# Another table of ranks for the list scheduler of an attention and two feed-forward blocks

## Chip, cores and metric

The kernel runs on one core of one Trainium2 chip, as one launch. The metric is the device time of one execution in microseconds (us); lower is better. TensorE (PE) does the matrix products, ScalarE (ACT), VectorE (DVE) and GpSimd (POOL) everything elementwise, and SyncE (SP) issues most of the DMAs.

## The reference, cut to what matters

Three stages follow each other. B=4 batches, H=8 heads, S=1152 positions, D=64; after attention the 4 x 576 rows of 512 numbers go through two feed-forward blocks.

```
q_pool = q.reshape(B, H, 576, 2, D).mean(axis=3)
p      = softmax(q_pool @ k.T / sqrt(D))
x      = (p @ v) as [2304, 512]
y      = (s * relu(x @ w_in) ** 2 + b) @ w_out               # 512 -> 2048 -> 512
out    = (sigmoid(y @ w_gate) * (y @ w_val)) @ w_out2        # 512 -> 1536 -> 512
```

The weights arrive as 64-bit floats (two 32-bit words each), everything else as 32-bit floats.

## The kernel before, in words

Products are made to keep the precision of 32-bit floats: an operand is split into a "hi" part that TensorE takes whole and a "lo" part, the rest. So nearly every product has a hi and a lo operation ahead of it on ACT, DVE or POOL, and a feed-forward product is three matmuls (lines 538 to 540: hi*hi, hi*lo, lo*hi).

Batch 0's attention is done by rows (`pair_rows`; operations named "r ...", prepared by "pr ..."): scores with queries on the partitions, row maximum and exponential from PSUM, then transposes of the probabilities. Batches 1 to 3 are done by columns (`pair_half`; prepared by "ps ..."). There one head's half goes through this chain: nine score products "qk" (line 768), for each a copy to SBUF "s copy" on ACT and a running maximum "s max" on DVE, three transposes "max T" (line 781), the reduction "max" (DVE, line 785), its way back to rows "max rows" (PE, line 746), three times "s - max" (DVE) and "exp" (ACT, line 794), the split "p hi" (ACT or POOL, lines 462 and 464) and "p lo" (DVE or POOL, line 472), and the products with v: "pv hi" (lines 816 and 817, six matmuls) and "pv lo" (line 821).

The first feed-forward block (`ffn1`) runs batch by batch: "ff xx up", "ff relu", "square", "g hi", "g lo", "ff down", "ff y add". For batch 0 its weights are decoded from 64-bit words: "w load" (DMA), "w top" (POOL or DVE), "w scale" (ACT), "w low", "w join", "w sign" (DVE), "w hi" (ACT or POOL), "w lo" (DVE or POOL). The result is kept in DRAM ("w keep"), and batches 1 to 3 fetch it by a DMA that POOL issues ("w fetch", line 520). The second block (`ffn2`: "p2 yy up", "gate", "gate val", "h hi", "h lo", "down 2", "out", "out add", "out store") handles two batches at a time, opens once the last attention tile is stored ("turn"), and decodes its weights both times. It stands in the order ffn2 of batches 0 and 1, ffn1 of batch 3, ffn2 of batches 2 and 3.

The order of all of it is made on the host, before the launch, by a list scheduler (`Plan`). Each operation is added with its engine (or a choice of two engines), an assumed duration, what it reads and writes, the buffers it needs, and a rank. `Plan.order` then runs an assumed clock: whenever an engine is free, it takes, among the operations on it whose inputs are ready and whose buffers fit, the one with the lowest rank. The program is issued in the order that comes out, and each engine then executes its own list strictly in that order.

```
FE, DE, AT, SK, FP = 0, 0.5, 1, 2, 3
...
up, on = self.moved.get(name, (0, 0))
self.ops.append([alts, None, issue, (rank + up, i + on), after, slots, port])
...
for item in items:
    if at[item[1]] <= now and (best is None or item < best) and fits(ops[item[1]]):
```

`rank` is one of the five constants: FE for the elementwise work of the feed-forward blocks, DE for decoding in ffn1 (FE in ffn2), AT for attention up to the exponentials, SK for what follows them, FP for feed-forward products. To it the table `MOVED` adds its first number for that name; its second shifts the place in program order that breaks ties. `self.moved` is that table. Operations that may run on either of two engines ("p hi", "p lo", "w lo", "g hi" and others) go to the one that reaches them first.

Of the kernel before, what the change touches and what calls it, by code (L numbers as in the profile page):

```python
# [25 lines left out]
    w=4, raw=3, xy=2, xx=1, r=2, g=4,  # L26
    qn=1, kn=1, vn=1, qT=2, kT=2, vt=2, st=6, pp=6,
    sg=2, mx=2, mc=2, r9=1, x=1, s=2, rs=1, rr=1,
    yy=1, yl=1, h=4, fo=9,
    ps=4, pr=8, pm=1, acc=5, ff=6, p2=3, bank=8,  # L30
# [5 lines left out]


MOVED = {
    "q load": (-0.5, 114),
    "k load": (46, 79),  # L40
    "v load": (58.5, 89),
    "v hi": (-18, -97),
    "v lo": (60, -156),
    "q add": (0, -97),
    "q twice": (0, -7),
    "pr qT": (0, 53),
    "pr q hi False": (23, -93),
    "pr q lo False": (24.5, 3),
    "pr q hi True": (45.5, 50),
    "pr q lo True": (5, 36),  # L50
    "pr kT": (-5, 44),
    "pr k hi": (2, -112),
    "pr k lo": (-5, 116),
    "s b load": (15, 94),
    "r qk 1": (0, 35),
    "r max": (36, 97),
    "r - max": (-29, -40),
    "r exp": (60, -57),
    "r pT": (-23, 13),
    "r p": (0, 52),  # L60
    "r p hi": (17, -107),
    "r p lo": (-25.5, -51),
    "r pv": (-38, 107),
    "r pT hi": (0, 70),
    "r pT lo": (47, -75),
    "r o": (-40, 39),
    "r x add": (40, -62),
    "r qk 2": (-1.5, -71),
    "r sums": (0.5, 106),
    "r sums eps": (-4, 9),  # L70
    "r 1 / sums": (-8, 75),
    "r spread": (-38, 44),
    "r rows": (0, -92),
    "r rows mid": (0, 108),
    "r x / sums": (-1.5, 74),
    "r x / sums mid": (60, 35),
    "r end": (0, 96),
    "ps qT": (24, 13),
    "ps q hi False": (60, 90),
    "ps q lo False": (6, -123),  # L80
    "ps kT": (10, 16),
    "ps k hi": (36.5, -29),
    "ps k lo": (-1, 88),
    "xx hi": (58, -86),
    "xx lo": (2.5, 93),
    "w load": (-12, 6),
    "w top": (-17, 81),
    "w scale": (-3, 17),
    "w low": (-20.5, -68),
    "w join": (9, 116),  # L90
    "w sign": (-25.5, -42),
    "w hi": (-40, 42),
    "w lo": (-28.5, -87),
    "w keep": (-1, 29),
    "one": (-39, -96),
    "ff xx up": (58, 135),
    "ff relu": (0, 72),
    "square": (-40, 76),
    "g hi": (27.5, -76),
    "g lo": (-10.5, 98),  # L100
    "ff down": (57, 43),
    "ff y": (9, 84),
    "column sum": (0, -65),
    "ff y add": (15.5, 115),
    "bias": (13.5, -34),
    "y bias": (-3, 137),
    "y store": (-33, -12),
    "qk": (44.5, 68),
    "s copy": (34.5, 24),
    "s max": (14, 33),  # L110
    "max T": (0, 53),
    "max": (20.5, 103),
    "max rows": (41.5, -120),
    "s - max": (14.5, 67),
    "exp": (0, -7),
    "p hi": (-40, -44),
    "p lo": (-7.5, -102),
    "pv hi": (-10.5, -118),
    "pv lo": (49.5, -31),
    "sums": (41, -60),  # L120
    "x": (36.5, 0),
    "sums out": (10, -13),
    "sums in": (5, -102),
    "1 / sums spread": (-16.5, 16),
    "1 / sums out": (60, -32),
    "1 / sums in": (2.5, -82),
    "x / sums": (0, 63),
    "1 / sums": (27.5, -20),
    "w fetch": (-35.5, -18),
    "w come": (-20.5, 6),  # L130
    "x store": (44, -24),
    "turn": (20, -21),
    "yy load": (-40, -79),
    "yy hi": (0, 50),
    "yy lo": (0, -39),
    "p2 yy up": (4.5, 6),
    "gate": (8, -90),
    "gate val": (-25.5, -72),
    "h hi": (0.5, 90),
    "h lo": (-40, -43),  # L140
    "down 2": (-21, 31),
    "out": (-5, -6),
    "out add": (0, -59),
    "out store": (-2, 45),
    "xx load": (0, 48),
    "p2 xx up": (0, -49),
    "p2 relu": (0, -7),
    "p2 down": (0, 24),
    "p2 y": (-10, -68),
    "p2 y add": (40, -54),  # L150
}


# [991 lines left out]
```

## Time and profile before

| | us |
|---|---|
| median of 3 runs | 1452.34 (1451.93 to 1453.6) |
| the profiled execution's own time | 1457.94 |
| its span, first to last instruction | 1456.2 |
| TensorE matmul busy | 1381.1 (95%) |
| VectorE, ScalarE, GpSimd busy | 1069.8, 936.4, 762.1 |
| mean granted TensorE clock | 0.990 of full speed |

The trace covers one execution, so its numbers are set against 1457.94 us and not against the median. Work is counted as busy time of each engine; "idle before, and what ended it" is the time an engine stood before an instruction, and the instruction of another engine that released it. In the tables by stretch each engine has its busy time and, in brackets, its instructions; PEclk is the granted clock as a share of 2.4 GHz.

### The profile page before, as it was taken

The page shows a single profiled execution, that of the slowest core. Times are in us where ns is not written, and L with a number is a line of the kernel's source. Part 1 is how long each engine was busy: PE and PEld are TensorE (multiplying, and loading weights), DVE is VectorE, ACT ScalarE, POOL GpSimd, SP SyncE. Part 2 cuts the span into 40 slices and gives each one's busy share as a digit, 9 for nine tenths or more (in the row PEclk, how much of TensorE's full clock was granted, in tenths as well). Part 3 has the DMA queues.
Part 4 walks back from the last instruction along what each step waited for, and adds up shares of the span by engine and source line. Part 5 has one row for each costly group of instructions (what it writes and reads, how often), then busy time and mean ns, then how long its engine had stood idle before and what let it go on. Part 6 is the DMA issues. An engine that isn't in the chain of part 4 may idle for free.

```text
span 1456.2 us, 24999 instructions
## 1 busy us (share of the span) xinstructions
PE 1381.1 (95%) x9164; PEld 1315.3 (90%) x9164; DVE 1069.8 (73%) x1780; ACT 936.4 (64%) x2004; POOL 762.1 (52%) x664
## 2 busy tenths in 40 slices
PE   7988999888999999999999989999999999999998
PEld 6877989887888999999899989999898999989897
DVE  6899899888998889889998856747475126738552
ACT  6899889778798999888888735434141534434130
POOL 3678577667776557565755434525353004526230
PEclk9999999999999999999999999999999999999999
DMA  3336134454433342233341363312236444313112
GB/s 90 93 121 200 31 101 124 155 157 149 154 109 136 87 140 75 84 103 121 95 140 42 121 260 131 101 59 87 73 100 230 163 172 145 117 48 126 34 69 65
DMA packets 103043, 167.88 MB, mean 115 GB/s; under 512 B 44652, under 2 KB 80264, under 8 KB 93832
## 3 DMA queue, kind: packets, MB, share of 16 engines
q1 hardware_dynamic: 96008, 115.95, 25.9%
q0 software_dynamic: 6912, 50.33, 9.8%
q8 instruction: 72, 1.18, 0.3%
q14 instruction: 51, 0.42, 0.1%
HBM read 139.99 MB, written 26.28 MB: 114 GB/s over the span
## 4 chain that ended last, share of the span: by engine, by line
PE 50%; ACT 8%; DVE 4%; issue 3%; DMA 2%; POOL 2%; SPq 0%; DVEq 0%; POOLq 0%; ACTq 0%
PE banks L538 11%; PE banks L540 11%; PE banks L539 11%; PE banks L1047 3%; PE banks L1048 3%; PE banks L1046 3%; PE banks L768 3%; ACT st L794 2%; PE banks L816 1%; ACT st L469 1%; PE banks L821 1%; PE banks L817 1%; DVE mx L475 1%; ACT pp L462 1%; DMA w<-d_1u_1u 1%
## 5 line engine op out<-in xcount | busy, mean ns | idle before, releaser
L472 POOL TENSOR_TENSOR pp<-st,pp 128x864 fp32r<-128x864 f32 x82 | 174.9, 2137 | 42.4 <-ACT pp L462 31.6
L540 PE MATMUL banks<-yy,w 128*128 128x384 f32 x576 | 192.6, 334 | 0.3 <-POOL w L472 0.3
L538 PE MATMUL banks<-yy,w 128*128 128x384 f32 x576 | 192.5, 334 | 0.0
L539 PE MATMUL banks<-yy,w 128*128 128x384 f32 x576 | 192.5, 334 | 0.0
L469 ACT COPY st<-banks 128x288 f32<-128x288 f32 x432 | 151.3, 409 | 39.9 <-PE banks L768 32.4
L768 PE MATMUL banks<-qT,kT 128*128 128x288 f32 x864 | 161.4, 304 | 3.2 <-DVE mx L475 2.7
L475 DVE TENSOR_TENSOR mx<-banks,mx 128x288 f32<-128x288 f32 x336 | 150.7, 449 | 18.1 <-ACT st L469 7.0
L538 PE MATMUL banks<-xx,w 128*128 128x288 f32 x512 | 155.1, 303 | 8.1 <-DMA w<-d_1u_1u 5.1
L539 PE MATMUL banks<-xx,w 128*128 128x288 f32 x512 | 152.4, 298 | 0.0
L540 PE MATMUL banks<-xx,w 128*128 128x288 f32 x512 | 152.4, 298 | 0.0
L475 DVE TENSOR_TENSOR st<-st,banks 128x864 f32<-128x864 f32 x144 | 148.9, 1043 | 2.4 <-PE banks L746 1.5
L538 PE MATMUL banks<-g,w 128*128 128x288 f32 x448 | 135.1, 302 | 3.3 <-DVE mx L475 2.1
L794 ACT ACTIVATE st<-st 128x864 f32<-128x864 f32 x144 | 132.0, 927 | 7.0 <-DVE st L475 6.4
L496 POOL TENSOR_SCALAR raw<-raw 128x512 f32<-128x512 f32 x99 | 77.4, 782 | 109.1 <-DMA raw<-in_moe_w_out_dram 40.6
L816 PE MATMUL banks<-pp,vt 128*128 128x288 f32 x432 | 123.6, 306 | 11.0 <-ACT pp L462 7.3
L768 PEld LDWEIGHTS banks<-qT,kT 128*128 128x128 f32 x864 | 127.9, 190 | 6.0 <-DVE mx L475 4.2
L539 PE MATMUL banks<-g,w 128*128 128x288 f32 x448 | 132.5, 296 | 0.0
L540 PE MATMUL banks<-g,w 128*128 128x288 f32 x448 | 132.5, 296 | 0.0
L817 PE MATMUL banks<-pp,vt 128*64 128x288 f32 x432 | 119.8, 297 | 0.0
L499 ACT ACTIVATE raw<-raw 128x512 f32<-128x512 f32 x104 | 71.1, 685 | 71.8 <-POOL raw L496 66.0
L540 PEld LDWEIGHTS banks<-yy,w 128*128 128x128 f32 x576 | 108.1, 188 | 0.6 <-POOL w L472 0.6
L538 PEld LDWEIGHTS banks<-yy,w 128*128 128x128 f32 x576 | 108.1, 188 | 0.3
(147 smaller groups left out, 3952.4 us busy)
## 6 DMA issues: line engine op xcount, KB each, us to landing
w<-d_1u_1u POOLq DMA_DIRECT2D x24, 1024.0 KB, 5.6
w<-d_1d_1d POOLq DMA_DIRECT2D x24, 1024.0 KB, 6.6
raw<-in_moe_w_out_dram SPq DMA_DIRECT2D x40, 512.0 KB, 3.9
raw<-in_moe_w_gate_dram SPq DMA_DIRECT2D x24, 512.0 KB, 12.7
raw<-in_moe_w_val_dram SPq DMA_DIRECT2D x24, 512.0 KB, 3.8
qn<-in_q_dram SPq DMA_DIRECT2D x16, 576.0 KB, 3.7
kn<-in_k_dram SPq DMA_DIRECT2D x32, 288.0 KB, 3.9
vn<-in_v_dram SPq DMA_DIRECT2D x32, 288.0 KB, 2.8
```

Source lines behind the costliest of these rows:

```text
L469: act(name, n, lambda: nc.scalar.copy(out=out(), in_=in_()), r, w, rank, sbuf=False)
L472: shared(name, n, lambda e: ENGINE[e].tensor_tensor(out=out(), in0=in0(), in1=in1(), op=op), r, w, rank, 2.15)
L475: dve(name, n, lambda: nc.vector.tensor_tensor(out=out(), in0=in0(), in1=in1(), op=op), r, w, rank)
L496: shared("w top", 512, lambda e: ENGINE[e].tensor_scalar(out=words(1).bitcast(F32), in0=words(1).bitcast(F32), scalar1=F64_TOP, scalar2=-F ...
L499: act("w scale", 512, lambda: nc.scalar.mul(words(1).bitcast(F32), words(1).bitcast(F32), 2.0 ** -112), [], [top], rank)
L538: nc.tensor.matmul(ps(), lhsT=whi(), rhs=xhi(), start=first, stop=False)
L539: nc.tensor.matmul((ps_lo or ps)(), lhsT=whi(), rhs=xlo(), start=False, stop=False)
L540: nc.tensor.matmul(ps(), lhsT=wlo(), rhs=xhi(), start=False, stop=last)
L768: nc.tensor.matmul(ps.t[:, :HQ], lhsT=kT.t[:, c], rhs=qq[:, w, hf * HQ:(hf + 1) * HQ], start=(w == 0), stop=(w == 1))
L794: act("exp", 3 * HQ, lambda s=s: nc.scalar.activation(out=s.t, in_=s.t, func=AF.Exp), [], parts, AT)
L816: nc.tensor.matmul(acc.t[:, :HQ], lhsT=vt.t[:, 3 * i + c, D:], rhs=hi.t[:, c], start=(i == c == 0), stop=False)
L817: nc.tensor.matmul(acc.t[:D, :HQ], lhsT=vt.t[:, 3 * i + c, :D], rhs=hi.t[:, c], start=False, stop=False)
```

## The change

All 112 entries of `MOVED` get other numbers; nothing else in the file changes. The same operations with the same tiles, engines to choose from and assumed durations go through the same scheduler, which may put them in another order and give an operation with a choice to the other engine. The entries that the prediction speaks of:

```diff
-    "pr k lo": (-5, 116),
+    "pr k lo": (-24, -69),
-    "ps q lo False": (6, -123),
+    "ps q lo False": (14.5, 47),
-    "ps kT": (10, 16),
+    "ps kT": (-1, 40),
-    "ps k hi": (36.5, -29),
+    "ps k hi": (23.5, -20),
-    "xx lo": (2.5, 93),
+    "xx lo": (29, 103),
-    "w load": (-12, 6),
+    "w load": (-40, -115),
-    "w lo": (-28.5, -87),
+    "w lo": (-31, 33),
-    "ff xx up": (58, 135),
+    "ff xx up": (60, -47),
-    "ff down": (57, 43),
+    "ff down": (33.5, 15),
-    "ff y add": (15.5, 115),
+    "ff y add": (18.5, 36),
-    "qk": (44.5, 68),
+    "qk": (15, -59),
-    "s copy": (34.5, 24),
+    "s copy": (28, 30),
-    "s max": (14, 33),
+    "s max": (11, -75),
-    "max T": (0, 53),
+    "max T": (-40, 58),
-    "max": (20.5, 103),
+    "max": (39, 59),
-    "s - max": (14.5, 67),
+    "s - max": (32, 49),
-    "p hi": (-40, -44),
+    "p hi": (-17.5, -87),
-    "pv hi": (-10.5, -118),
+    "pv hi": (-32.5, -57),
-    "pv lo": (49.5, -31),
+    "pv lo": (32, 66),
-    "1 / sums": (27.5, -20),
+    "1 / sums": (-5, 0),
-    "w fetch": (-35.5, -18),
+    "w fetch": (-34, 14),
-    "yy load": (-40, -79),
+    "yy load": (0, 68),
-    "xx load": (0, 48),
+    "xx load": (-3, 54),
...
```

## Rows read from the trace of the kernel before

**Rows 1.** The profile's first two lines: the span, and busy time by engine.

```profile
span 1456.2 us, 24999 instructions
...
PE 1381.1 (95%) x9164; PEld 1315.3 (90%) x9164; DVE 1069.8 (73%) x1780; ACT 936.4 (64%) x2004; POOL 762.1 (52%) x664
```

**Rows 2.** Busy time by stretch, with granted clock and DMA.

```profile
core 0: us, PE busy (x) PEld busy (x) DVE busy (x) ACT busy (x) POOL busy (x), PEclk, DMA share, GB/s
0.00:40.00 40.00, 29.86 (x181) 26.92 (x181) 26.40 (x61) 26.82 (x79) 14.56 (x26) 0.96 0.31 82
40.00:480.00 440.00, 395.35 (x2825) 370.53 (x2825) 391.59 (x735) 379.47 (x886) 312.68 (x274) 0.98 0.41 129
480.00:840.00 360.00, 350.12 (x2611) 339.19 (x2611) 315.06 (x513) 309.79 (x642) 212.21 (x157) 1.00 0.32 100
840.00:880.00 40.00, 36.22 (x262) 36.02 (x261) 20.75 (x30) 14.57 (x27) 15.52 (x16) 0.96 0.64 241
880.00:1440.00 560.00, 558.27 (x3243) 533.30 (x3242) 312.13 (x436) 205.19 (x370) 207.09 (x193) 1.00 0.33 109
1440.00:1456.20 16.20, 11.33 (x53) 9.38 (x51) 3.88 (x6) 0.51 (x1) 0.00 (x0) 0.96 0.35 81
```

**Rows 3.** What TensorE waited for: us in total, times, longest us.

```profile
PE banks L816 <- ACT pp L462: 7.3, 10, 2.0
PE banks L746 <- DVE mc L785: 7.2, 8, 2.7
PE banks L702 <- ACT qn L462: 6.7, 1, 6.7
...
PE banks L538 <- DMA w<-d_1u_1u: 5.1, 2, 3.8
PE banks L538 <- DVE mx L475: 4.3, 2, 2.2
PE banks L816 <- POOL pp L464: 3.4, 3, 1.5
PE banks L781 <- DVE mx L475: 2.9, 6, 1.1
PE banks L768 <- DVE mx L475: 2.7, 4, 1.0
PE banks L702 <- DVE kT L475: 2.5, 4, 1.4
...
PE banks L966 <- DVE kT L475: 1.8, 2, 1.0
```

**Rows 4.** GpSimd's groups in 200 to 420 us: busy, mean ns, idle before.

```profile
L472 POOL TENSOR_TENSOR w<-raw,w 128x512 fp32r<-128x512 f32 x16 | 24.0, 1508 | 9.1 <-ACT w L462 9.0
...
L464 POOL TENSOR_SCALAR pp<-st 128x864 fp32r<-128x864 f32 x9 | 9.9, 1100 | 7.3 <-ACT st L794 7.3
```

**Rows 5.** Groups of VectorE, whole span.

```profile
L475 DVE TENSOR_TENSOR st<-st,banks 128x864 f32<-128x864 f32 x144 | 148.9, 1043 | 2.4 <-PE banks L746 1.5 <-ACT st L469 0.9
...
L725 DVE SCALAR_TENSOR_TENSOR qT<-banks,qT 128x256 fp32r<-128x256 f32 x64 | 23.8, 415 | 4.8 <-ACT qT L722 4.5
```

**Rows 6.** TensorE by stretch of 4 us, where it stood and after.

```profile
256.00:260.00 4.00, 1.44 (x9) 1.00 0.72 293
260.00:264.00 4.00, 3.38 (x15) 0.57 0.05 13
...
856.00:860.00 4.00, 0.22 (x2) 1.00 1.05 419
```

**Rows 7.** Stretches of 20 us, all engines.

```profile
300.00:320.00 20.00, 16.49 (x115) 15.71 (x115) 16.08 (x27) 14.88 (x25) 15.80 (x16) 0.95 0.60 202
320.00:340.00 20.00, 14.99 (x103) 14.23 (x103) 14.80 (x26) 17.77 (x39) 15.40 (x11) 0.93 0.43 136
...
360.00:380.00 20.00, 17.27 (x112) 15.82 (x112) 19.32 (x39) 11.89 (x26) 12.69 (x14) 0.91 0.70 223
```

**Rows 8.** Stretch of 40 us with the second block's 512-wide products.

```profile
920.00:960.00 40.00, 40.00 (x213) 36.74 (x212) 21.24 (x31) 14.06 (x25) 14.66 (x14) 1.00 0.22 66
```

More of the change, by code (lines that the diff above doesn't have):

```diff
@@ L38 @@
 MOVED = {
[L39 to L52, printed above, removed]
-    "pr k lo": (-5, 116),
[L54 to L76, printed above, removed]
@@ L77 @@
-    "r end": (0, 96),
-    "ps qT": (24, 13),
-    "ps q hi False": (60, 90),
-    "ps q lo False": (6, -123),
-    "ps kT": (10, 16),
-    "ps k hi": (36.5, -29),
-    "ps k lo": (-1, 88),
-    "xx hi": (58, -86),
-    "xx lo": (2.5, 93),
-    "w load": (-12, 6),
[L87 to L92, printed above, removed]
-    "w lo": (-28.5, -87),
-    "w keep": (-1, 29),
-    "one": (-39, -96),
-    "ff xx up": (58, 135),
@@ L97 @@
[L97 to L100, printed above, removed]
-    "ff down": (57, 43),
-    "ff y": (9, 84),
-    "column sum": (0, -65),
-    "ff y add": (15.5, 115),
-    "bias": (13.5, -34),
-    "y bias": (-3, 137),
-    "y store": (-33, -12),
-    "qk": (44.5, 68),
-    "s copy": (34.5, 24),
-    "s max": (14, 33),
-    "max T": (0, 53),
-    "max": (20.5, 103),
-    "max rows": (41.5, -120),
-    "s - max": (14.5, 67),
-    "exp": (0, -7),
-    "p hi": (-40, -44),
@@ L117 @@
-    "p lo": (-7.5, -102),
-    "pv hi": (-10.5, -118),
-    "pv lo": (49.5, -31),
[L120 to L127, printed above, removed]
-    "1 / sums": (27.5, -20),
-    "w fetch": (-35.5, -18),
-    "w come": (-20.5, 6),
-    "x store": (44, -24),
-    "turn": (20, -21),
-    "yy load": (-40, -79),
-    "yy hi": (0, 50),
-    "yy lo": (0, -39),
@@ L136 @@
[L136 to L144, printed above, removed]
-    "xx load": (0, 48),
[L146 to L150, printed above, removed]
+    "q load": (-5, 84),
+    "k load": (0, 18),
+    "v load": (60, 113),
+    "v hi": (0, 144),
+    "v lo": (24.5, 78),
@@ new lines @@
+    "q add": (-11, 0),
+    "q twice": (0, -53),
+    "pr qT": (0, 70),
+    "pr q hi False": (20, 58),
+    "pr q lo False": (-2, -53),
+    "pr q hi True": (21.5, 41),
+    "pr q lo True": (-1, 142),
+    "pr kT": (0, -86),
+    "pr k hi": (8, 90),
+    "pr k lo": (-24, -69),
+    "s b load": (-6, -118),
+    "r qk 1": (0, 5),
+    "r max": (27, 83),
+    "r - max": (-40, 0),
+    "r exp": (53, -23),
+    "r pT": (-34, -58),
+    "r p": (0, -44),
+    "r p hi": (16.5, 38),
+    "r p lo": (-21, -145),
@@ new lines @@
+    "r pv": (-40, -136),
+    "r pT hi": (3, -93),
+    "r pT lo": (49, 88),
+    "r o": (0, -102),
+    "r x add": (44, -86),
+    "r qk 2": (-33, 63),
+    "r sums": (0, -3),
+    "r sums eps": (-1.5, 53),
+    "r 1 / sums": (-30, 107),
+    "r spread": (-14, -11),
+    "r rows": (-9.5, -67),
+    "r rows mid": (0, 70),
+    "r x / sums": (41, -20),
+    "r x / sums mid": (60, 79),
+    "r end": (11.5, -68),
+    "ps qT": (4, 116),
+    "ps q hi False": (44, -128),
+    "ps q lo False": (14.5, 47),
@@ new lines @@
+    "ps kT": (-1, 40),
+    "ps k hi": (23.5, -20),
+    "ps k lo": (0, -8),
+    "xx hi": (26, 35),
+    "xx lo": (29, 103),
+    "w load": (-40, -115),
+    "w top": (-12, -106),
+    "w scale": (-0.5, -54),
+    "w low": (-22, -118),
+    "w join": (2, -117),
+    "w sign": (-37, 42),
+    "w hi": (-40, -26),
+    "w lo": (-31, 33),
+    "w keep": (-40, 8),
+    "one": (-31.5, 2),
+    "ff xx up": (60, -47),
+    "ff relu": (-2, 3),
+    "square": (-40, 37),
+    "g hi": (11.5, 61),
+    "g lo": (-8, -23),
@@ new lines @@
+    "ff down": (33.5, 15),
+    "ff y": (9, -129),
+    "column sum": (-5, 13),
+    "ff y add": (18.5, 36),
+    "bias": (14.5, -130),
+    "y bias": (-1.5, -36),
+    "y store": (21, 45),
+    "qk": (15, -59),
[3 more added lines that the diff above has]
+    "max": (39, 59),
+    "max rows": (7.5, -46),
+    "s - max": (32, 49),
+    "exp": (5, 102),
+    "p hi": (-17.5, -87),
+    "p lo": (0, -32),
+    "pv hi": (-32.5, -57),
+    "pv lo": (32, 66),
+    "sums": (36.5, -50),
@@ new lines @@
+    "x": (35, 76),
+    "sums out": (-8, 62),
+    "sums in": (-25.5, 24),
+    "1 / sums spread": (0, 100),
+    "1 / sums out": (21, 98),
+    "1 / sums in": (8, 55),
+    "x / sums": (0.5, 181),
+    "1 / sums": (-5, 0),
+    "w fetch": (-34, 14),
+    "w come": (-22.5, -41),
+    "x store": (-3, -20),
+    "turn": (1, -178),
+    "yy load": (0, 68),
+    "yy hi": (-1.5, 25),
+    "yy lo": (-20, -85),
+    "p2 yy up": (1.5, 8),
+    "gate": (0, -24),
+    "gate val": (-40, -76),
+    "h hi": (9, 96),
@@ L151 @@
+    "h lo": (-38.5, -99),
+    "down 2": (-1, 62),
+    "out": (0, 33),
+    "out add": (-2, -136),
+    "out store": (24, -131),
+    "xx load": (-3, 54),
+    "p2 xx up": (0, -87),
+    "p2 relu": (13, -100),
+    "p2 down": (0, -3),
+    "p2 y": (0, 16),
+    "p2 y add": (0, 21),
 }
```

## The prediction

> **What bounds the kernel now.** I read the page's first lines, then busy time by stretch, then TensorE's waits, and then the lists of VectorE and GpSimd in the stretch where those waits lie. Matmuls take 1381.1 of 1456.2 us [rows 1]: TensorE is the bound, and its own work is the same in any order. What an order can change is the 75 us in which it stands. They are not spread evenly [rows 2]: 10.1 in the first 40 us, 44.7 in 40 to 480, 9.9 in 480 to 840, 3.8 in 840 to 880, 1.7 in the 560 us after that and 4.9 at the end. From 880 us on the second block keeps TensorE full (558.27 of 560), whatever the ranks say. So the change is decided in 40 to 480 us, where attention and the decoding of the first block's weights fill VectorE (391.59 of 440, 89%) and ScalarE (379.47, 86%), and feed-forward products, the only filler, are short because their weights are still being decoded. The waits there are small ones [rows 3]: "pv hi" for "p hi" 7.3 us from ACT and 3.4 from POOL, "max rows" for "max" 7.2, three groups that wait for "s max" 4.3, 2.9 and 2.7. The 6.7 of the first q load and the 4.9 of the last store no rank moves.
>
> **How far the order really changes.** The scheduler compares ranks only between operations of one engine that are ready together, so I added constant and table entry for each name and compared pairs, over the whole table. Among the names of the column stage the order turns round in 1 of 36 pairs on TensorE, 7 of 120 on ScalarE, 28 of 171 on VectorE (11 of them by "1 / sums" alone, from 29.5 to -3) and 13 of 120 on GpSimd. On TensorE "qk" (45.5, then 16), "pv lo" (51.5, then 34), "ff down" (60, then 36.5) and "ff xx up" (61, then 63) keep their sequence, so attention still goes first and the feed-forward products still fill. In the second block no pair of TensorE turns. The new table is a close relative of the old one; what follows prices the pairs that turn at a place where TensorE waits. Where an operation moves ahead of what held it up I take half of the wait that it ends: nothing is the one end (the operation ahead is then behind it, on an engine that is 89% busy), the whole wait the other.
>
> 1. "ps q lo" falls from 7 to 15.5, behind "s max" (15, then 12), and "ff y add" and "s - max", which were level with "s max" at 15.5, move off to 18.5 and 33. So the running maximum, which frees the score banks, no longer queues behind up to 415 ns of "ps q lo" [rows 5]. Waits for it: 4.3 + 2.9 + 2.7 = 9.9 us [rows 3]; half is -4.95. Ends: 0 and -9.9.
>
> 2. The next pair's keys come earlier: "pr k lo" from -4 to -23, "ps kT" from 11 to 0 and "ps k hi" (37.5, then 24.5) past "s copy" (35.5, then 29). TensorE waited 2.5 + 1.8 = 4.3 us for kT [rows 3]; half is -2.15. Ends: 0 and -4.3.
>
> 3. "max T" goes from 1 to -39 and so past "pv hi" (-8.5, then -30.5), which shortens the way to "max"; but "max" itself falls from 21.5 to 40 on VectorE, with "xx lo" (2.5, then 29) now ahead, and "s - max" still ahead at 1043 ns each [rows 5]. Both act on the 7.2 us of "max rows" [rows 3]. I take 0; at most 7.2 either way.
>
> 4. "p hi" loses its place at the top: -38, then -15.5. On ScalarE only decoding and "square" stood ahead of it and still do. On GpSimd "w lo" (-28, then -30.5) is now ahead. In 200 to 420 us GpSimd did 9 "p hi" and 16 "w lo" at 1508 ns, 24.0 us or 11% of the stretch [rows 4]. With twice that share as the chance that a "w lo" is ready just then, 9 x 0.22 x 1.5 = 3.0 us later "p hi"; filler covers about half of it, as TensorE is short of it in this stretch only: +1.5. Ends: 0 and 9 x 1.508 = +13.6, if each one waits and nothing covers it.
>
> 5. "w fetch" (-35.5, then -34) also passes "p hi". The wait for it was 5.1 us in 2 places, 3.8 in one [rows 3], the one at 856 to 860 us, where the DMA engines were full (1.05) [rows 6]. At that turn "yy load" (-40, then 0) drops behind three "w load" (-12, then -40) and "xx load", but the bytes that collide with the fetch are the same, and TensorE has the last products of ffn1 to run until about 880 us (36.22 of 40) [rows 2]. I take 0; -5.1 if the collision goes, as much the other way if it doubles.
>
> Decoding keeps its place ahead of "s max" on every engine, and the tail has one kind of work in the queue; both count 0.
>
> Sum: -4.95 - 2.15 + 1.5 = -5.6 us. The profiled execution would go from 1457.94 to 1452.3. That execution lies 5.6 us above the median of the runs, so against the median the forecast is 1452.34 - 5.6 = 1446.7 us.
>
> [...]
>
> **The rivals.**
>
> No difference that can be told (1452). VectorE and ScalarE are 89% and 86% busy in 40 to 480 us, their work is fixed, and the pairs that turn are few: a wait that goes at one place comes back at the next. For it speaks that many small groups make up the idle time and none is above 7.3 us; against it that GpSimd stands at 312.68 of 440 [rows 2], so that there is an engine to move work to. This is also the case in which the table does not do what a table can, change the sequence where it counts.
>
> Slower, 1463. Step 4 decides: "p hi" starts the only way from the exponentials to "pv hi", and TensorE waits for it more than for anything else, 10.7 us [rows 3]. If 6 of the 9 on GpSimd wait out a whole "w lo" in the stretch without filler, that is 9.0 us, and one such hole that grows costs clock as well: in 256 to 260 us TensorE was busy for 1.44 of 4 us, and in the next 4 us the granted clock was 0.57 [rows 6], between the two levels of 1.2 and 2.4 GHz, so 0.43 of 4 us of work, 1.7, was lost. 9.0 + 1.7 = +10.7. The point from which this outweighs the gains: 7.1 / 1.5 = five of them uncovered. Against it: ScalarE, where nothing new is ahead of "p hi", can take it.
>
> A large gain, 1437. The worst holes lie in 300 to 340 and 360 to 380 us, where TensorE stood 3.5 + 5.0 + 2.7 = 11.2 us, and the clock fell to 0.95, 0.93 and 0.91 of full there, which over 20 us each loses another 1.0 + 1.4 + 1.8 = 4.2 us of work [rows 7]. If the new sequence happens to bring decoded weights in time for these, 15.4 us go. The Trainium skill's page TensorE: Matmul & The Clock Gate, section HAM oscillation, has it that a gap in TensorE's work is paid twice, once as idle time and once as half clock after it; the stretch of 0.57 above agrees. Against it: no rank of decoding changes its place.
>
> **How the numbers follow.** The forecast, a small gain between 1440 and 1449.4, has a chance of 0.36; the large gain 0.09; no difference 0.25; slower 0.30. What can't be told from no change is 0.2%, 2.9 us either side. So faster is 0.45, same 0.25, slower 0.30. The range takes the whole of steps 1, 2 and the fetch at the low end, 1452.3 - 19.3 = 1433, and at the high end step 4 whole with no gain, 1452.3 + 13.6 = 1466.
>
> **What would show it.** In the changed kernel's profile: TensorE's busy time about the same, and its idle time in 40 to 480 us down from 44.7 to about 39; waits for "s max" (mx) near 5 us, for kT near 2; waits of "pv hi" for "p hi" at 10 to 13. Step 4 is wrong if those do not grow while GpSimd does more "p hi". The whole is wrong if the stretch after 880 us grows, if holes appear in 480 to 840 us, where I took nothing, or if the sequence at the turn of 840 to 880 us costs more than the 3.8 us that stand there now.

## The result, and the profile after

The changed kernel takes 1463.61 us (median of 4 runs, 1461.13 to 1467.72), the kernel before 1452.97 in the same runs (4, 1451.93 to 1455.87). The ratio is 1.0073, with a 95% interval of 1.0045 to 1.01: slower by 10.6 us, where 5.6 us less had been forecast. The profiled execution took 1467.72 us, 9.8 more than the one of before.

The span and the busy time, as in [rows 1]:

```profile
span 1465.9 us, 25015 instructions
...
PE 1383.9 (94%) x9164; PEld 1318.5 (90%) x9164; DVE 1075.4 (73%) x1778; ACT 934.5 (64%) x2001; POOL 773.1 (53%) x669
```

The same 9164 matmuls are busy for 2.8 us more, which is work at a lower granted clock (0.985 of full speed in the mean, 0.990 before). The span grew by 9.7, so the other 6.9 us are idle time of TensorE. Where they lie is seen in the busy time by stretch, in the columns of [rows 2]:

```profile
0.00:40.00 40.00, 29.46 (x190) 26.51 (x191) 27.54 (x64) 27.96 (x83) 15.55 (x28) 1.00 0.31 82
40.00:480.00 440.00, 399.59 (x2852) 376.94 (x2851) 398.62 (x742) 385.73 (x896) 323.55 (x278) 0.97 0.41 130
480.00:840.00 360.00, 344.65 (x2548) 331.53 (x2547) 307.57 (x499) 302.56 (x629) 210.78 (x155) 0.99 0.31 99
840.00:880.00 40.00, 36.33 (x264) 36.13 (x263) 18.69 (x31) 12.90 (x23) 11.70 (x14) 0.96 0.60 219
880.00:1440.00 560.00, 552.81 (x3221) 529.55 (x3220) 316.59 (x435) 203.85 (x369) 211.54 (x197) 0.99 0.33 109
1440.00:1465.90 25.90, 21.11 (x100) 17.88 (x98) 6.38 (x10) 1.52 (x3) 0.00 (x0) 0.96 0.31 72
```

Against [rows 2], idle time is +0.4 us up to 40 us, -4.2 in 40 to 480 (44.65 to 40.41, near the 39 hoped for), +5.5 in 480 to 840, -0.1 at the turn, +5.5 in 880 to 1440 and -0.1 at the end: 6.9 in sum. What gain there is stands where it was looked for; how sure it is comes further down. The loss is in the two stretches where the prediction took nothing.

TensorE's waits, as in [rows 3]:

```profile
PE banks L781 <- DVE mx L475: 11.3, 11, 4.2
PE banks L538 <- DMA w<-d_1u_1u: 10.9, 2, 7.2
PE banks L816 <- ACT pp L462: 6.7, 7, 1.8
...
PE banks L702 <- DVE kT L475: 4.6, 5, 2.3
PE banks L746 <- DVE mc L785: 4.4, 11, 1.0
PE banks L816 <- POOL pp L464: 2.7, 4, 0.9
PE banks L966 <- DVE kT L475: 1.8, 2, 1.0
PE banks L768 <- DVE mx L475: 1.0, 1, 1.0
PE banks L538 <- DVE mx L475: 0.6, 1, 0.6
```

The last figure of a line, its longest single wait, matters most here: 7.2 and 4.2 us stand out. Both are followed by a stretch at half clock, as the granted clock (third figure from the right) by 4 us shows:

```profile
628.00:632.00 4.00, 0.55 (x5) 0.86 0.75 260
632.00:636.00 4.00, 3.21 (x14) 0.50 0.27 76
...
1140.00:1144.00 4.00, 0.00 (x0) 0.86 1.09 421
1144.00:1148.00 4.00, 1.39 (x6) 0.50 1.05 422
```

**The hole at 1140 us.** Some names first: the raw val and raw gate loads are the "w load" of `w_val` and `w_gate`; y of batch 2 goes to DRAM by the y store and comes back, by the yl load ("yy load"), as the tile yl; d_1u and d_1d are the kept up and down weights that GpSimd fetches. The timeline of the kernel after, of SyncE, VectorE, GpSimd and TensorE in turn; in square brackets is the idle time before an instruction and what ended it:

```profile
1102.99 0.38 SPq L491 DMA_DIRECT2D raw<-in_moe_w_val_dram  x1
1104.15 0.37 SPq L491 DMA_DIRECT2D raw<-in_moe_w_gate_dram  x1
1104.58 0.50 SPq L658 DMA_DIRECT2D y_d<-xy  x1
1107.74 15.19 SPq L1061 DMA_DIRECT2D out_dram<-fo  x6
1123.03 0.53 SPq L549 DMA_DIRECT2D yl<-y_d  x1
...
1116.33 0.43 DVE L500 TENSOR_SCALAR raw<-raw 128x512 uint32<-128x512 uint32 x1 [8.62 <-DMA raw<-in_moe_w_gate_dram]
...
1129.72 1.32 POOL L464 TENSOR_SCALAR yy<-yl 128x576 fp32r<-128x576 f32 x2 [12.46 <-DMA yl<-y_d]
1130.99 3.86 POOL L472 TENSOR_TENSOR yy<-yl,yy 128x576 fp32r<-128x576 f32 x2
1134.80 1.15 POOL L520 DMA_DIRECT2D w<-d_1d_1d  x2
1135.93 0.55 POOL L520 DMA_DIRECT2D w<-d_1u_1u  x1
...
1146.61 0.58 PE L538 MATMUL banks<-xx,w 128*128 128x288 f32 x1 [7.19 <-DMA w<-d_1u_1u]
```

The same place in the kernel before:

```profile
1099.52 0.38 SPq L491 DMA_DIRECT2D raw<-in_moe_w_val_dram  x1
1099.95 0.50 SPq L658 DMA_DIRECT2D y_d<-xy  x1
1106.85 0.34 SPq L549 DMA_DIRECT2D yl<-y_d  x1
1107.29 0.50 SPq L491 DMA_DIRECT2D raw<-in_moe_w_gate_dram  x1
1107.84 19.59 SPq L1061 DMA_DIRECT2D out_dram<-fo  x18
...
1123.08 0.61 POOL L520 DMA_DIRECT2D w<-d_1d_1d  x1 [1.45 <-PE banks L1048]
...
1130.79 0.53 POOL L520 DMA_DIRECT2D w<-d_1u_1u  x1 [5.82 <-PE banks L540]
...
1138.17 0.37 PE L538 MATMUL banks<-xx,w 128*128 128x288 f32 x1 [1.32 <-DMA w<-d_1u_1u]
```

Read it as a chain. In the new order the raw gate load stands ahead of the y store (ranks: "w load" -12 to -40, "y store" -33 to 21). It goes out at 1104.15, right behind the first of two fetches of 1 MB that GpSimd issues, and lands at 1116.3, 12 us later. VectorE has the decoding of that load at its head and stands 8.62 us, so the out adds come late. The first six out stores, which wait for them, stand on SyncE ahead of the yl load, which leaves at 1123.03, 20.0 us behind the raw val load; before it was 7.3. GpSimd has the split of yl at its head and stands 12.46 us, and behind that split are the fetches of the next feed-forward weights. So two fetches of down weights and one of up weights leave within 1.2 us, where before the up weights left 7.7 us behind the first down weights. The DMA engines are full (1.09, then 1.05), and TensorE goes on 10.7 us after the fetch of up weights was issued (7.4 before). It has run dry for 7.2 us and comes back at half clock. The x load and the turn at 840 to 880 us, which step 5 looked at, have no part in it. Which of the new entries makes this order was not run one by one. "yy load" alone does not explain the place of the yl load: its rank falls from -40 to 0, but that of "out store" falls further, from -2 to 24.

**The hole at 628 us** has the same shape:

```profile
611.94 0.60 POOL L520 DMA_DIRECT2D w<-d_1d_1d  x1
613.48 0.53 POOL L520 DMA_DIRECT2D w<-d_1d_1d  x1 [0.94 <-PE banks L540]
...
624.71 2.31 POOL L472 TENSOR_TENSOR qn<-qn 128x576 f32<-128x576 f32 x1 [6.52 <-DMA qn<-in_q_dram]
...
629.59 2.69 DVE L472 TENSOR_TENSOR g<-r,g 128x576 fp32r<-128x576 f32 x1 [3.50 <-POOL g L464]
```

A q load issued at 613.33 us beside two fetches lands at 624.7, 11.4 us later. GpSimd stands before "q add" (rank 1 to -10); "g hi" behind it is late, VectorE stands before "g lo", "s max" behind that is late, and "max T" on TensorE waits 4.24 us.

### The profile page after: what moved, and what is told of

Read it like the earlier page. It is cut to its first block, busy times and chain, and to the rows that moved or that the text cites. A ratio compares the mean times of both kernels' runs of the same rounds, so it can differ in the third digit from the quotient of the medians.

```text
span 1465.9 us, 25015 instructions
## 1 busy us (share of the span) xinstructions
PE 1383.9 (94%) x9164; PEld 1318.5 (90%) x9164; DVE 1075.4 (73%) x1778; ACT 934.5 (64%) x2001; POOL 773.1 (53%) x669
## 4 chain that ended last, share of the span: by engine, by line
PE 64%; ACT 13%; DVE 9%; DMA 5%; issue 5%; POOL 3%; SPq 0%; ACTq 0%; DVEq 0%; POOLq 0%
PE banks L538 13%; PE banks L540 13%; PE banks L539 13%; PE banks L768 4%; PE banks L1048 3%; PE banks L1047 3%; PE banks L1046 3%; PE banks L816 3%; PE banks L817 2%; ACT st L794 2%; PE banks L821 2%; ACT st L469 2%; ACT kT L469 2%; PE banks L966 2%; DVE mx L475 2%
## 5 line engine op out<-in xcount | busy, mean ns | idle before, releaser
L472 POOL TENSOR_TENSOR pp<-st,pp 128x864 fp32r<-128x864 f32 x86 | 185.1, 2156 | 36.7 <-ACT pp L462 33.1
L538 PE MATMUL banks<-xx,w 128*128 128x288 f32 x512 | 156.1, 305 | 11.8 <-DMA w<-d_1u_1u 10.9
L500 DVE TENSOR_SCALAR raw<-raw 128x512 uint32<-128x512 uint32 x104 | 67.2, 649 | 59.1 <-DMA raw<-in_moe_w_gate_dram 24.8
L538 PEld LDWEIGHTS banks<-xx,w 128*128 128x128 f32 x512 | 98.6, 193 | 13.0 <-issue 7.4
```

The costliest lines, as they stand in the source:

```text
L472: shared(name, n, lambda e: ENGINE[e].tensor_tensor(out=out(), in0=in0(), in1=in1(), op=op), r, w, rank, 2.15)
L538: nc.tensor.matmul(ps(), lhsT=whi(), rhs=xhi(), start=first, stop=False)
```

## The experiments

All ratios are to the kernel before, run beside each one on the same chip; 0.001 is 1.45 us. Most kernels move a few operations in the finished order and touch nothing else:

```diff
-        for i in self.order():
+        order = self.order()
+        for i, j in MOVES:            # operation i goes right behind j
+            order.remove(i)
+            order.insert(order.index(j) + 1, i)
+        for i in order:
```

**e1_yl_ahead**, from the kernel after: the yl load goes right behind the y store, ahead of the out stores.

```diff
+MOVES = ((6857, 4633),)    # yy load behind y store
```

> The changed kernel with one operation moved in the finished order: the load of y of batch 2 for the second block stands right behind the store of that y on SyncE, ahead of the six DMAs of out rows that stood before it. Only SyncE's list differs. Theory A (an in-order engine stands before a DMA that lands late): the load is issued some 10 us earlier than at 1123 us, GpSimd gets past its split of y and issues the weight fetches earlier, the wait of TensorE at 1139 us falls from 7.2 us to under 2, and the half clock after it (3.4 us of work) goes too: 1463.6 - 8 = about 1455.5 us. Rival B (the DMA engines are full there, the fetch comes late whatever the order): the hole stays, 1462 to 1464. Rival C (step 4 of the prediction: 'p hi' behind 'w lo' on GpSimd makes the kernel slower): no change, 1463.6.

Measured 1.0045 [1.0029, 1.0062], some 4 us of the 8 expected, with an interval that overlaps that of the change. The hole's wait falls from 7.2 to 2.8 us, and no half clock follows it. It does not vanish, since the store itself, issued at 1100.86 behind the gate load and 0.5 us behind the first of the two fetches, lands only at 1115.75 (14.9 us; in the kernel before 6.9), and the yl load can't go sooner.

**e2_q_add_behind**, from the kernel after: "q add" and "q twice" go behind "v lo" of the same stretch.

```diff
+MOVES = ((4744, 4089), (4745, 4744))    # q add behind v lo, q twice behind q add
```

> The changed kernel with 'q add' and 'q twice' of one pair (the one that GpSimd waits 6.5 us for at 618 to 624.7 us) moved behind the five other operations that stood after them on GpSimd; their transposes come some 35 us later. Only GpSimd's list differs. Theory A: the gap of 4.2 us in TensorE at 628 us and the half clock after it (3.4 us) go: 1463.6 - 4 to - 7, about 1458 us. Rival B (attention is bound by the work of VectorE and ScalarE, a wait that goes comes back at the next place): under 2 us, 1462 to 1464. Rival C ('p hi'): no change, 1463.6.

Measured 1.0052 [1.0035, 1.007]. The hole at 628 us is gone (idle in 480 to 840 us 15.3 to 11.4, no half clock there), the late one stays at 7.5 us. By ratio (1.0073 - 1.0052) this hole is some 3 us of the loss, less than the 4 to 7 of theory A, but the two intervals overlap, so that this pair alone does not tell it from nothing. A surer pair are e5 and e6 below, which differ by this move only: 1.0021 and 0.9992, 4.2 us, with intervals that do not meet. The hole also differs between executions of one order: up to 1090 us the change, e1 and e5 are the same, and yet the wait of "max T" there is 4.24, 2.87 and 0.6 us, and only the first has half clock behind it.

**h1_late_of_before** and **h2_late_of_after** use one table for operations numbered below 5565 and the other above: h1 the new one first, h2 the old one first.

```diff
-        up, on = self.moved.get(name, (0, 0))
+        up, on = (self.moved if i < SPLIT else LATER).get(name, (0, 0))
```

> The new table for every operation up to the turn, the table of before for the operations behind it (second block and the first block's last batch). Theory A: the attention half's hole at 628 us stays, the one at 1139 us goes: 1463.6 - 7 = about 1456 us. If the loss lies wholly in attention ('p hi' and the like): 1463. If it lies wholly behind the turn: 1453.

> The reverse: the table of before up to the turn, the new table behind it. Theory A: the order of stores and loads behind the turn is that of the new table, so the hole in TensorE before the first block's last batch comes in: 1453 + 7 = about 1460 us. If the loss lies wholly in attention: 1453. Since the plan behind the turn starts from another point, the hole may differ in size; A is wrong if there is no late load of y ahead of it.

Measured 1.0122 [1.0105, 1.0139] and 1.0027 [1.0013, 1.004]: both missed. The split is by number, and the y store (4633) got its rank from the other table than the out stores. In h1 it fell behind four of them, the yl load left 21.8 us behind the raw val load, and TensorE's wait was 8.8 us, longer than in the change. In h2 the store went ahead of the out stores but behind the gate load: 16.4 us, a wait of 3.6. As a split into "early" and "late" the pair failed. It did show a larger hole where the yl load leaves later behind the raw val load.

**e5_store_first**, from the kernel after: the y store and its yl load go ahead of the raw gate load, as they stood before.

```diff
+MOVES = ((4633, 6882), (6857, 4633))    # y store behind raw val load, yy load behind it
```

> The changed kernel with SyncE's order around 1100 us as the kernel before had it: first the store of y of batch 2, then its load for the second block, then the weight load that stood ahead of both, then the out rows. Nothing else moves. With the load alone moved ahead (e1_yl_ahead) the store still took 14.9 us to land, because a weight load of 512 KB and two fetches of 1 MB ran beside it, and a wait of 2.8 us stayed. Theory A: the store lands in some 7 us, the hole shrinks to 1.5 us and no half clock follows it: 1463.6 - 9 = about 1454.5 us, 3 less than e1. Rival B (the two fetches alone slow the store): as e1, 1457.7.

Measured 1.0021 [1.0005, 1.0037]. The store lands in 7.0 us, the yl load leaves 7.4 us behind the raw val load, the wait is 1.5 us, and there is no half clock after 880 us, as theory A had it. By ratio (1.0073 - 1.0021) the late hole is some 7.5 us of the loss, and the two intervals do not meet.

**e6_both_holes** is e5 and e2 together.

> e5_store_first and e2_q_add_behind together. If the two holes are the whole of the loss and independent, the gains add: 1463.6 - 9 - 4.9 = about 1449.7 us, below the kernel before. If one feeds the other (less filler left behind, so the later hole opens again), only the larger shows: about 1454.5.

Measured 0.9992 [0.998, 1.0004]. With two turns of order put back, out of a whole table, the loss is gone: 11.8 us by ratio, where e5 and e2 alone make 7.5 and 3, so the gains add. Its busy time in the two stretches that had lost:

```profile
480.00:840.00 360.00, 348.83 (x2594) 335.65 (x2593) 309.86 (x503) 302.33 (x625) 210.71 (x157) 1.00 0.33 109
...
880.00:1440.00 560.00, 557.43 (x3219) 532.33 (x3218) 316.75 (x437) 197.82 (x359) 208.65 (x193) 1.00 0.32 105
```

TensorE is back to 348.83 and 557.43 us, against 344.65 and 552.81 in the change and 350.12 and 558.27 in [rows 2]. So the two holes are the cause, and the rest of the new table is worth -1.2 us, with an interval that holds zero.

**f1_x_load_later**, e6 with one more turn: the x load at the turn goes behind the second yl load.

```diff
+MOVES = (..., (6448, 5575))    # xx load behind second yy load
```

> e6_both_holes, and the load of x of batch 3 (1152 KB, wanted only after 890 us) moved from the head of SyncE's list at the turn, 834 us, behind the second load of y at 855 us. In both kernels a hole of 3 to 4 us in TensorE stands at 856 to 864 us, with the DMA engines full from 844 on. Theory A: 1.2 MB less ahead of the fetches there is some 3 us at the 400 GB/s that the profile shows, and the hole goes with the half clock behind it: 3 to 5 us less than e6, about 1445.5 us. Rival B: the other loads fill the same engines just as much, no change against e6.

Measured 1.0021 [1.0007, 1.0035], a miss: some 4 us more than e6. TensorE's longest wait at the turn is 4.5 us (2.8 in e6), and the granted clock in 840 to 880 us falls to 0.91 (0.96 in e6). GpSimd stands 5.26 us for the third raw load of the turn, but its next fetch is released by TensorE, 4.22 us after GpSimd was done, so that this load is not what delays it. The fetch of up weights that TensorE waits for leaves at 847.43; the second yl load and the x load now leave right behind it, at 848.5 and 848.93, and TensorE goes on 10.5 us after its issue (8.9 in e6). That these two loads slow it is read from the order of times and was not tried.

**b1_x_load_later**, the same move in the kernel before.

> The kernel before with one turn of SyncE moved: the xx load that stands ahead of the second yy load goes behind it. If the first holes at the turn of the feed-forward part (840 to 880 us, 3.8 us idle in before) come from the order of those two loads, 1 to 3 us faster; if, as in the earlier run of the same move on the kernel after, the loads behind are only re-timed, the same or up to 5 us slower, with a longer wait for a fetched weight at 840 to 880 us.

Measured 0.9968 [0.9953, 0.9982]: it beats both kernels, 4.6 us under before, more than the 1 to 3 us of its better case. Its stretch at the turn:

```profile
840.00:880.00 40.00, 38.70 (x285) 38.50 (x284) 21.25 (x31) 20.50 (x37) 17.52 (x18) 1.00 0.73 264
```

and all its waits for a fetched up weight:

```profile
PE banks L545 <- DMA w<-d_1u_1u: 1.3, 1, 1.3
```

Idle time at the turn falls from 3.8 to 1.3 us and its half clock is gone (0.96 to 1.00). The wait of 1.3 us that is left is the one at the turn, at 853.84; the late one of [rows 3] is not in the list, and at 1130 us TensorE stands 1.24 us for ScalarE. Here the second yl load and the x load leave over 5 us behind the fetch of up weights (846.48, then 851.78 and 852.23), and TensorE goes on 7.4 us after its issue. One move gave -4.6 in one order and about +4 in another, so what it is worth depends on the order around it, by these times on which transfers it meets.

**b2_gate_load_first** puts the suspected cause into the kernel before: its raw gate load goes ahead of the y store.

```diff
+MOVES = ((6926, 6882),)    # raw gate load behind raw val load
```

> The kernel before with one turn of SyncE moved: the raw gate load of the expert weights goes ahead of the y store, as it stands in the kernel after, and nothing else is touched. Theory (the hole after 880 us is made on SyncE, by what is sent between the raw val load and the yl load): the y store, the raw gate load and the two fetches of 1 MB are under way together, the store takes about 15 us to land in place of 6.9, the yl load is issued some 15 to 17 us behind the raw val load in place of 7.3, TensorE's longest wait for a fetched expert weight goes from 1.3 to about 3 us, and the time is 2 to 5 us over before. Rival (the hole needs the other queues' new order as well, the out stores ahead of yl above all): yl still comes early enough, the wait stays under 2 us and the time within 1.5 us of before.

Measured 1.0031 [1.0013, 1.005]. SyncE's timeline:

```profile
1099.14 0.38 SPq L498 DMA_DIRECT2D raw<-in_moe_w_val_dram  x1
1101.23 0.37 SPq L498 DMA_DIRECT2D raw<-in_moe_w_gate_dram  x1
1101.65 0.50 SPq L665 DMA_DIRECT2D y_d<-xy  x1
1115.09 0.34 SPq L556 DMA_DIRECT2D yl<-y_d  x1
```

and what TensorE waited for in 1100 to 1160 us:

```profile
PE banks L545 <- DMA w<-d_1u_1u: 3.0, 1, 3.0
```

The store now takes 13.4 us to land, the yl load leaves 16.0 us behind the raw val load, and the wait is 3.0 us in place of 1.3. The theory said 15 to 17, about 3, and 2 to 5 us over; 4.5 were measured. In this execution 2.1 us of it are idle time in 880 to 1440 us, and behind the wait the granted clock falls to 0.57 for 4 us. One load ahead of the y store on SyncE is enough for a loss, with every other queue as before; the rest of the 7.2 us comes with the out stores ahead of yl, which b2 and e1 (2.8 us) have behind it.

**b3_p_hi_alone**: the kernel before with one entry of the new table, "p hi".

```diff
-    "p hi": (-40, -44),
+    "p hi": (-17.5, -87),
```

> The kernel before with one entry of the new table, p hi at (-17.5, -87). Theory (p hi is not what costs the change its time): TensorE's waits for p hi stay between 9 and 12 us (10.7 before, 9.4 after) and the time stays within 3 us of before. Rival (the prediction's case of p hi behind p lo and w lo on GpSimd, priced there at a time near 1463): these waits grow by 8 us or more, and the time is 8 us or more over before. The scheduler's own plan ends 4.7 us later with this entry alone.

Measured 1.0083 [1.0061, 1.0104]: as much lost as by the whole table, and neither expectation in full. Its waits of "pv hi" for "p hi", and of "max T":

```profile
PE banks L816 <- ACT pp L462: 13.1, 14, 2.5
PE banks L781 <- DVE mx L475: 7.0, 5, 5.6
...
PE banks L816 <- POOL pp L464: 2.4, 3, 1.2
```

and VectorE's timeline at that last wait of 5.6 us:

```profile
541.24 0.46 DVE L472 TENSOR_TENSOR xy<-xy,rr 128x288 f32<-128x288 f32 x1 [6.32 <-DMA rr<-r_d]
```

Waits for "p hi" grow from 10.7 to 15.5 us, +4.8, less than the 8 the rival wanted. The rest is a third hole of the same shape: VectorE reaches the product that needs the transfer rr with nothing left to do ahead of it and stands 6.32 us, "max T" waits 5.6, and the clock falls to 0.51 behind it. In the kernel before that instruction starts at 541.58, no sooner, with 0.26 us of standing. So the entry alone is bad, but in the whole table, where waits for "p hi" are 9.4, the others take it back (e6 has this entry too, and stands at 0.9992): what an entry costs does not add up.

**x1_other_ties**: the first numbers of before with the second numbers of after.

```diff
-    "q add": (0, -97),
+    "q add": (0, 0),
...
```

> The first numbers of the table of before with the second numbers, those that break ties, of the new table. If the first numbers carry what a table is worth, as the prediction took it when it counted the pairs that turn, this runs like the kernel before, 1449 to 1457 us. If a table is worth something only as the one sequence that both columns were chosen for, it is much slower: the scheduler's own assumed clock ends at 1433 us with it, 34 later than at 1399 with the table of before (and at 1393 with the new one), which would be about 1487 us.

Measured 1.0238 [1.0214, 1.0261], about +35 us, as the second case had it, with all ranks as before and only the tie-breakers new. TensorE's idle time in 40 to 480 us is 53.8 us in place of 44.7.

**h3_late_store_first** is h2 with the two moves of e5.

> The table of before up to the second block's feed-forward operations and the table of after behind them (as in the earlier run at 1.0027), with the y store and its yl load moved ahead of the raw gate load. Theory (that run's loss is the same hole, at its mild size): the longest wait for a fetched expert weight falls from about 3 us to under 2, and the time is at before, 0 to 4 us under the earlier run by ratio, 0.9985 to 1.001. Rival (the late half of the new table costs time elsewhere): the ratio stays at 1.002 or above with the hole gone.

Measured 1.0019 [0.9998, 1.0039], which tells neither side apart from h2. The yl load leaves after 7.5 us, but the wait stays; SyncE's timeline, and then TensorE's wait in 1110 to 1160 us:

```profile
1105.08 28.20 SPq L1185 DMA_DIRECT2D out_dram<-fo  x18
```

```profile
PE banks L662 <- DMA w<-d_1u_1u: 3.5, 1, 3.5
```

Its 18 out stores are spread over 28.2 us (19.6 before), so that they lie beside the fetch that TensorE waits for; e6, where they take 27.6, keeps 2.6 us. But in e5 they take 27.3, and the wait is 1.5. What makes these last 2 us stays open.

The late hole over the kernels: how long behind the raw val load the yl load leaves, how long behind the first fetch of down weights the fetch of up weights leaves, and TensorE's longest wait for a fetched weight there.

| kernel | yl behind raw val, us | up behind down weights, us | wait, us |
|---|---|---|---|
| before, e5, e6, h3 | 7.3, 7.4, 7.4, 7.5 | 7.7, 7.2, 7.0, 7.3 | 1.3, 1.5, 2.6, 3.5 |
| b1 | 7.4 | 7.7 | none |
| b2, h2, e1 | 16.0, 16.4, 16.5 | 4.0, 2.7, 2.8 | 3.0, 3.6, 2.8 |
| after, e2, h1 | 20.0, 20.4, 21.8 | 1.1, 1.1, 1.1 | 7.2, 7.5, 8.8 |

Only the last row stands apart, the one where the three fetches leave together. Between the others a difference of 1 us says little: e5 and e6 have the same order there, with 1.5 and 2.6.

## Why the prediction was wrong

**"From 880 us on the second block keeps TensorE full, whatever the ranks say"** is the sentence that failed. It read a full stretch as one that can't lose. TensorE is full there because a chain over two in-order lists, SyncE's (y store, yl load) and GpSimd's (split of yl, fetch), comes just in time: in [rows 3] its wait is 1.3 us. The new ranks make the chain 12.7 us longer, and the stretch lost 5.5 us of idle time, and half clock behind it. The prediction named this very loss as what would prove it wrong.

**480 to 840 us** was put at nothing as well. "q add" (1, then -10) is priced in no step; its place cost some 3 to 4 us there (e2, and e5 against e6).

**Step 5** named two of the entries at work ("yy load" behind "w load"), but not "y store" (-33, then 21) and "out store" (-2, then 24), and looked at the turn only, where the wait stayed as it was (3.8, then 3.7). The y of batch 2 comes back for the second block at 1100 us, and there the new order of these operations cost the most. "The bytes that collide with the fetch are the same" was true and beside the point: what changed is which transfer goes out behind the fetches, and which engine has the operation that needs it at its head.

**How far the order changes.** First numbers and pairs were counted; x1 shows that a change of the second numbers alone can cost 35 us. "A close relative" was no argument. That no pair of TensorE turns said nothing of the queues that feed it.

**Step 1** forecast waits for "s max" of 5 us; they rose from 9.9 to 12.9. Without the 4.24 of the hole at 628 us they are 8.7, so at most 1.2 of the 4.95 came. "ff y add" and "s - max" (15.5) were not level with "s max" (15) but already behind it, so that their move freed nothing.

**Step 2** forecast 2 us for kT; it rose from 4.3 to 6.4. Moving the keys' operations up was not enough to have them early.

**Step 3** took 0 within 7.2 either way; the wait for "max" fell from 7.2 to 4.4, within its bounds. "xx lo" was ahead of "max" in both tables (2.5 against 21.5, 29 against 40), not only now.

**Step 4** forecast +1.5 on the waits for "p hi"; in the whole table they fell by 1.3. Alone, in b3, they grow by 4.8, inside the bounds of 0 to 13.6. The direction was right for the entry and wrong for the table. The two are not quite the same case: alone, "p hi" (-15.5) falls behind "w top" (-16.5) too, which the new table puts at -11.5. And its sign of being wrong is met by half: the waits did not grow, but GpSimd did 42 "p hi" before and after, no more.

**The rivals.** The one that said 1463 had the time by chance and not the cause: it put 9.0 us into waits for "p hi", and these fell. By the same chance the time lies inside the range: its high end was step 4 whole, a cost that did not come. What that rival had right is the second half of its price, that a hole in TensorE's work can cost clock behind it: the granted clock is 0.50 behind both holes of the change. The Trainium skill's page TensorE: Matmul & The Clock Gate, section HAM oscillation, describes it for waits on a DMA, behind which the next products start at the lower clock. The 7.2 us at 1140 us agree; behind the 2.9 and 2.8 us of e1 the granted clock stays at 1.00. The case of no difference is what e6 comes to once both holes are out. For the large gain nothing speaks.

The gain of 4.2 us in 40 to 480 us, and the loss of 5.5 in 480 to 840, are less sure than they look. The kernel before, b1 and b2 have the same order up to some 830 us, and in their executions TensorE stands 44.7, 42.2 and 41.0 us in the first of these stretches and 9.9, 11.8 and 12.5 in the second; in the change, e1 and e5 it stands 40.4, 39.7 and 40.4, and 15.4, 14.8 and 12.3. After 880 us the two orders are far apart: 1.7 and 1.7 us (before, b1) against 7.2 and 7.6 (the change, e2).

What is still open: whether the store of 1.1 MB lands late because of the two fetches that go out around it or because of the gate load ahead; where it lands late, both come together. Without the two together a load is late as well: the q load of the other hole has no gate load beside it, and in h1, where the y store leaves 15 us later, the gate load still takes 9.7 us.

## What to carry to other kernels

A stretch in which the bound engine is full is not safe from a new order: follow the chain that keeps it fed over every queue, and ask for each in-order engine which transfer the operation at its head needs, and what else is on the DMA engines when that transfer goes out. When order is all that changes, look at the longest single waits and not at sums of small ones: here two places in the order, four operations in all, cost what was lost. A single move of a load is worth what it meets, so try it in the kernel where it is to stay.

## What the runs showed of the hardware

How late a transfer lands depends on what left just ahead of it, more than had been allowed for. The y store of 1.1 MB took 6.9 to 7.0 us when it left ahead of two fetches of 1 MB (before, e5), and 13.4 to 14.9 when it left within 0.5 us behind the first of them, with the gate load of 0.5 MB (b2, h2, e1). That gate load itself took 12.2 to 12.6 us there (after, e1, h2), and one q load 9.1 to 11.4 us beside two such fetches (e1, e5, h1, after), where the median of all q loads of the change is 3.6. An engine that reached the operation waiting for such a transfer stood for 6.3 to 16.8 us (VectorE in b3, GpSimd in b2), and all that was behind it on its list waited too.

A wait of about 3 us in TensorE's work is followed by a lower granted clock in some executions and not in others: 0.57 behind 3.0 us in b2 and behind 2.6 in e6, 1.00 behind 2.9 and 2.8 in e1.
